# The middle of a decode kernel's feed-forward in two halves, and its second weight in other pieces

## The chip, the cores and the metric

One core of a Trainium2 chip. The metric is the device time of one execution in microseconds (us), the median of several executions. Inside one profiled execution I use a second, finer measure: times counted from the landing of the last part of w1 (the sixteenth semaphore increment of that transfer in the trace), because what the change touches begins there and the 345 us before it differ by some tenths from one execution to the next. These differences are taken in nanoseconds and then rounded; the recorded texts took some of them from rounded times and so stand 0.01 us off in places (1.57 for 1.58, 1.38 for 1.39).

## The reference, cut to what matters

One decode step: an attention block with a cached K and V of 8 heads x 32768 positions x 128 (134 MB in bfloat16, 32 query heads), an output projection, then a feed-forward block:

```python
h = _layernorm(x) * (1 + cb) + sb
x = x + gb * (relu(h @ w1) @ w2)      # w1: 512 x 1792, w2: 1792 x 512
```

The batch is one row, so the feed-forward is two products of one row with a matrix. w2 is 14 "rows" of 512 columns per partition (128 partitions x 14 = 1792); one such row is 128 KB.

Of the kernel before, what the change touches and what calls it, by code (L numbers as in the profile page):

```python
# [11 lines left out]
ACT = mybir.ActivationFunctionType  # L12
# [5 lines left out]
def kernel(  # L18
# [14 lines left out]
    nc = tc.nc  # L33
    P = 128
# [4 lines left out]
    KT = D // P  # L39
    Dff = B_w1.shape[1]  # L40
    FT = Dff // P
# [6 lines left out]
    WOROWS = 2  # L48
    LAST = Hkv - 1
    LOOPED = Hkv - 2  # L50
    W2P = [(0, 4), (4, 8), (8, 10), (10, 12), (12, 13), (13, 14)]
    W1P = [(0, KT - 1), (KT - 1, KT)]
    assert Dh == 128 and REP == 4 and D == 512 and FT == W2P[-1][1] and NTILE == 4
    scale = float(Dh) ** -0.5
# [36 lines left out]
    def piece(name, at, n):  # L91

        if name not in pieces:
            pieces[name] = ring.tile([P, 2 * TK * Dh], BF16, tag="slot", name=name)
        return pieces[name][:, at:at + n]

    def load(key):
# [23 lines left out]
        else:  # L121
            f0, f1 = W2P[key[1]]
            t = piece("w12_sb", KT * Dff + f0 * D, (f1 - f0) * D).rearrange("p (f d) -> p f d", d=D)
# [20 lines left out]
    stream += [("v", LAST, (0, 1)), ("v", LAST, (2,)), ("v", LAST, (3,))] + [("wo", i) for i in range(len(WOP))]  # L144
    stream += [("w1", i) for i in range(len(W1P))] + [("w2", i) for i in range(len(W2P))]
    pos = [0]

    def need(key):
        while key not in loaded:
            load(stream[pos[0]])  # L150
            pos[0] += 1
        return loaded[key]
# [17 lines left out]
    for hp in range(4):  # L170
# [9 lines left out]
        out=mask4, in_=ident_f[:].rearrange("p (x q) -> p q x", q=REP), op=ALU.add, axis=AX.X,  # L180
# [3 lines left out]
    for n in sorted({n * REP for _, n in WOP}):  # L184
        cmask[n] = const.tile([P, P // n], F32, name=f"cmask{n}")
        nc.vector.tensor_reduce(
            out=cmask[n][:], in_=ident_f[:].rearrange("p (c r) -> p c r", r=n), op=ALU.add, axis=AX.X,
# [3 lines left out]
            out=rsel_f[:], in_=ident_f[:].rearrange("p (c r) -> p r c", r=n), op=ALU.add, axis=AX.X,  # L191
# [6 lines left out]
        out=smask[:], in_=ident_f[0:16, 0:16].rearrange("p (s q) -> p s q", q=REP), op=ALU.add, axis=AX.X,  # L198
# [8 lines left out]
        out=place32[:], in_=ident_f[:].rearrange("p (j m) -> p m j", m=32), op=ALU.add, axis=AX.X,  # L207
# [3 lines left out]
        out=rowpick[:], in_=ident_f[:].rearrange("p (j m) -> p j m", m=32), op=ALU.add, axis=AX.X,  # L211
# [10 lines left out]
        out=cx_bd[:], in0=cx_row[:].unsqueeze(1).to_broadcast([16, 8, D // 8]),  # L222
# [17 lines left out]
    def bank(name):  # L240
        return ps_s.tile([P, 512], F32, tag="s", name=name)[:]
# [61 lines left out]
    def rows_sb(name):  # L303
        return spool.tile([P, 2, 512], F32, tag="S_g", name=name)
# [26 lines left out]
    def four_rows(e, name):  # L331
# [15 lines left out]
        out=nca[:], in0=modT_sb[:, KT:2 * KT], scalar1=-1.0, scalar2=-1.0, op0=ALU.mult, op1=ALU.add,  # L347
# [3 lines left out]
        out=ncb[:], in0=modT_sb[:, 4 * KT:5 * KT], scalar1=-1.0, scalar2=-1.0, op0=ALU.mult, op1=ALU.add,  # L351
# [16 lines left out]
    for i in range(2):  # L368
        nc.vector.transpose(out=q_cols[:, i, :], in_=q_ps[i])
        nc.scalar.copy(  # L370
            out=qT_sb[:, 16 * i:16 * (i + 1)], in_=q_cols[:, i, :].rearrange("p (h r) -> p h r", r=32)[:, :, 0],
# [223 lines left out]
    def keep_clock(n):  # L595

        if not spare:
            spare.append(bank("spare_ps"))
        for _ in range(n):
            nc.tensor.matmul(spare[0], lhsT=ident_bf[:], rhs=qbd[0][:, 0, 0:4, :], start=True, stop=True)  # L600

    with tc.manual_schedule(engines={mybir.EngineType.PE, mybir.EngineType.DVE}):
# [11 lines left out]
        for g in range(LAST):  # L614
# [58 lines left out]
        hid_ps = ps_o.tile([P, 512], F32, tag="o", name="hid_ps")  # L673
# [22 lines left out]
            out=x1T[:], in0=x1T[:], scalar=1.0, in1=xT, op0=ALU.mult, op1=ALU.add, accum_out=stat2[:, 0:1],  # L696
# [15 lines left out]
        NQ = 32 * FT  # L712
        for part, (k0, k1) in enumerate(W1P):
            w1_sb = need(("w1", part))
            for kt in range(k0, k1):
                for q in range(4):
# [2 lines left out]
                        rhs=w1_sb[:, kt - k0, q * NQ:(q + 1) * NQ], start=False, stop=(kt == KT - 1),  # L719
                        skip_group_check=True,  # L720
                    )
        keep_clock(4)
        hidT = rows_sb("hidT").rearrange("p a b -> p (a b)")[:, 0:NQ].rearrange("p (f e) -> p f e", e=32)
        nc.vector.transpose(out=hidT, in_=hid_ps[:, 0:NQ].rearrange("p (e f) -> p f e", f=FT))  # L724
        hb = hid_bd[:]
        nc.scalar.activation(  # L726
            out=AP(hb.tensor, hb.offset, [hb.ap[0], [KT * KT, FT], [KT + 1, KT]]),
            in_=hidT[:, :, 0:1].to_broadcast([P, FT, KT]), func=ACT.Relu,
        )

        ffn_ps = bank("ffn_ps")[0:KT, 0:P]
        for part, (f0, f1) in enumerate(W2P):
            w2_sb = need(("w2", part))
# [41 lines left out]
```

## The kernel before: the parts that the change touches

All of K, V and the weights run through one queue of transfers (Sync engine), in the order of use; wo, w1 and w2 come last. w2 comes in six pieces, each a transfer with its own semaphore:

```python
W2P = [(0, 4), (4, 8), (8, 10), (10, 12), (12, 13), (13, 14)]
...
stream += [("w1", i) for i in range(len(W1P))] + [("w2", i) for i in range(len(W2P))]
```

At the end the hidden row lies in PSUM on four partitions. Vector (DVE) turns it so that it lies along partitions, Scalar (ACT) applies the relu and writes the values on diagonals of a zeroed tile, and TensorE (PE) multiplies: four matmuls for each row of w2, 56 in all, into one accumulator. `keep_clock(n)` issues n unused matmuls that keep TensorE busy while it waits.

```python
keep_clock(4)
hidT = ...                                   # 128 x 448, in SBUF
nc.vector.transpose(out=hidT, in_=hid_ps[:, 0:NQ].rearrange("p (e f) -> p f e", f=FT))
nc.scalar.activation(out=AP(hb.tensor, hb.offset, [hb.ap[0], [KT * KT, FT], [KT + 1, KT]]),
                     in_=hidT[:, :, 0:1].to_broadcast([P, FT, KT]), func=ACT.Relu)
ffn_ps = bank("ffn_ps")[0:KT, 0:P]
for part, (f0, f1) in enumerate(W2P):
    w2_sb = need(("w2", part))
    for ft in range(f0, f1):
        for i in range(KT):
            nc.tensor.matmul(ffn_ps, lhsT=hid_bd[:, ft, i, :], rhs=w2_sb[:, ft - f0, i * P:(i + 1) * P], ...)
o_rows = ffn_ps * gb_rows; o_bf = o_rows + x1_rows     # two Vector operations, then the store (abridged)
```

## Time and profile before

| | before |
|---|---|
| time, median of the first 3 runs | 355.47 us (355.39 to 356.15) |
| span of the profiled execution | 353.3 us |
| w1's last landing | 345.62 us from the start |
| last of the 56 matmuls starts | 350.35 us |

The page and the chain of waits are shown in the prediction. Beside them, these are the instructions of the middle in order of time (start, length, engine, line, operation, count; in brackets the idle time before and what ended it; PEld is the loading of weights into TensorE):

```profile
346.07 0.65 DVE L724 STREAM_TRANSPOSE hidT<-hid_ps 128x448 f32<-128x448 f32 x1 [1.32 <-PE hid_ps L717]
346.82 0.33 ACT L726 ACTIVATE hid_bd<-hidT 128x56 bf16<-128x56 f32 x1 [2.71 <-DVE hidT L724]
347.19 3.19 PEld L736 LDWEIGHTS <-hid_bd 128*4 128x4 bf16 x56 [0.70 <-ACT hid_bd L726]
347.19 3.37 PE L736 MATMUL ffn_ps<-w_sb,hid_bd 128*4 128x128 bf16 x56 [0.20 <-ACT hid_bd L726]
```

The matmuls wait for ACT, ACT for DVE.

### The profile page before, as it was taken

Reading aid. Unit: us, or ns where it says so; the run is one execution under the profiler, and the core shown is the slowest. Engines: PE = TensorE matmul, PEld = TensorE weight load, DVE = VectorE, ACT = ScalarE, POOL = GpSimd, SP = SyncE. Lnnn points to the kernel's source line nnn. Section 1 sums busy time; section 2 is a strip of 40 time slices with the busy share of each in tenths; the row PEclk is TensorE's granted clock in tenths of the full one; section 3 lists DMA queues with packets and bytes.
Section 4 is the critical chain, followed back from the end, with each engine's and each line's share of the span. In section 5 each row is a group of like instructions: output and inputs, shape, how many; then the busy total and the mean of one; then the engine's idle time right before and its main releaser. Section 6 shows DMA issues by size and latency. Waiting matters only on the chain. (4 is left out here: it accounts for less than half of the span.)

```text
span 353.3 us, 3999 instructions
## 1 busy us (share of the span) xinstructions
PE 282.0 (80%) x1310; PEld 112.9 (32%) x1312; DVE 209.1 (59%) x270; ACT 28.3 (8%) x68; POOL 9.7 (3%) x16
## 2 busy tenths in 40 slices
PE   0273882899798979897989796979689797989996
PEld 0031331233233323332333232323234233334444
DVE  7737683963848467662939177553938095743141
ACT  1023004000110011001010101010100000011000
POOL 8200000000000000000000000000000000000000
PEclk9985888599899999998999999999969999999999
DMA  8999999999999999999999999999999999999995
GB/s 312 456 419 438 443 420 423 449 434 419 440 441 419 427 456 421 423 449 434 419 438 443 419 423 454 430 418 445 441 415 427 449 428 419 449 438 403 429 419 204
DMA packets 6852, 149.59 MB, mean 423 GB/s; under 512 B 824, under 2 KB 1080, under 8 KB 1976
## 3 DMA queue, kind: packets, MB, share of 16 engines
q1 hardware_dynamic: 6776, 149.43, 98.5%
q8 instruction: 8, 0.13, 0.1%
q14 instruction: 4, 0.03, 0.0%
q0 software_dynamic: 64, 0.00, 0.0%
HBM read 149.42 MB, written 0.00 MB: 423 GB/s over the span
## 5 line engine op out<-in xcount | busy, mean ns | idle before, releaser
L405 DVE STREAM_TRANSPOSE KTt<-Ksb 128x2048 f32<-128x2048 f32 x64 | 143.3, 2284 | 60.6 <-DMA Ksb<-in_A_k_cache_dram 50.4
L487 PE MATMUL o_ps<-Vsb,PT_g 128*16 (+1 forms) x512 | 129.2, 390 | 21.7 <-ACT qbd L389 9.7
L425 PE MATMUL S_ps<-KTt,qbd 128*128 128x512 bf16 x512 | 124.6, 396 | 17.0 <-DVE KTt L405 15.6
L425 PEld LDWEIGHTS <-qbd 128*128 128x128 bf16 x512 | 49.5, 99 | 83.2 <-issue 26.6
L487 PEld LDWEIGHTS o_ps<-Vsb,PT_g 128*16 x416 | 36.9, 89 | 90.2 <-issue 64.6
L431 DVE TENSOR_SCALAR_CACHE_REDUCE S_g<-S_ps 128x512 f32<-128x512 f32 x16 | 11.0, 690 | 30.5 <-PE S_ps L425 30.5
L389 ACT COPY qbd<-qrep_sb 32x128 bf16<-32x128 bf16 x32 | 9.4, 295 | 134.4 <-PE S_ps L425 133.3
L468 DVE STREAM_TRANSPOSE PT_g<-P_g 128x1024 bf16<-128x1024 bf16 x8 | 9.8, 1225 | 6.7 <-ACT P_g L462 6.6
L459 ACT ACTIVATE nbias<-Mb_ps 128x1 f32<-128x1 f32 x8 | 1.4, 171 | 133.1 <-PE Mb_ps L457 133.1
L227 PE MATMUL xc_ps<-cx_sel,cx_bd 16*128 16x2 bf16 x4 | 0.3, 172 | 14.5 <-DVE cx_bd L221 14.5
L487 PEld LDWEIGHTS <-PT_g 128*16 128x16 bf16 x96 | 8.2, 90 | 11.0
L462 ACT ACTIVATE P_g<-S_g,nbias 128x1024 bf16<-128x1024 f32 x8 | 9.2, 1149 | 0.2
L173 DVE COPY sel<-ident_bf 128x128 bf16<-128x128 bf16 x4 | 8.1, 3940 | 1.1 <-POOL ident_bf masks.py:199 1.1
L518 DVE SCALAR_TENSOR_TENSOR Y<-o_ps,smask,Y 16x128 f32<-16x128 f32 x24 | 8.1, 339 | 0.8
L474 PE MATMUL L_ps<-Lexp,ones_f 128*128 128x4 f32 x16 | 2.9, 254 | 4.3 <-DVE Lexp L471 4.3
L446 DVE TENSOR_REDUCE Mrow<-mT_ps 1x4 f32<-1x128 f32 x8 | 2.1, 257 | 7.1 <-PE mT_ps L443 7.1
L600 PE MATMUL spare_ps<-qbd,ident_bf 128*128 128x512 bf16 x18 | 5.4, 380 | 0.2 <-issue 0.2
L443 PE MATMUL mT_ps<-ident_f,m_p 128*1 128x128 f32 x8 | 2.2, 270 | 3.9 <-DVE m_p L440 2.0
L474 PEld LDWEIGHTS L_ps<-Lexp,ones_f 128*128 128x128 f32 x16 | 3.2, 221 | 5.8 <-issue 5.1
L227 PEld LDWEIGHTS <-cx_bd 16*128 16x128 bf16 x4 | 0.2, 114 | 14.5 <-DVE cx_bd L221 14.5
L537 DVE TENSOR_TENSOR oT_sb<-acc_ps,Linv 128x4 bf16<-128x4 f32 x8 | 1.2, 152 | 5.7 <-PE acc_ps L524 5.7
L295 PE MATMUL mod_ps<-wm_sb,siluT 128*1 128x512 bf16 x24 | 3.6, 624 | 1.1 <-DVE siluT L289 1.1
(115 smaller groups left out, 88.3 us busy)
## 6 DMA issues: line engine op xcount, KB each, us to landing
Ksb<-in_A_k_cache_dram SPq DMA_DIRECT2D x16, 4096.0 KB, 27.7
Vsb<-in_A_v_cache_dram SPq DMA_DIRECT2D x15, 4096.0 KB, 24.1
wq_sb<-in_A_wq_dram SPq DMA_DIRECT2D x1, 4096.0 KB, 19.3
Vsb<-in_A_v_cache_dram SPq DMA_DIRECT2D x2, 2048.0 KB, 23.3
wm_sb<-in_w_mod_dram SPq DMA_DIRECT2D x1, 3072.0 KB, 10.1
wo_sb<-in_A_wo_dram SPq DMA_DIRECT2D x1, 2048.0 KB, 24.9
w_sb<-in_B_w_dram SPq DMA_DIRECT2D x1, 1344.0 KB
wo_sb<-in_A_wo_dram SPq DMA_DIRECT2D x1, 1024.0 KB, 27.0
```

What stands on the lines that cost most here:

```text
L173: nc.vector.tensor_copy(out=sel[:, hp, :].rearrange("p (a c) -> p a c", a=4), in_=src)
L295: nc.tensor.matmul(dst[j // 4][32 * (j % 4):32 * (j % 4) + 1, :], lhsT=src_T[:, kt:kt + 1], rhs=w[:, kt, j * 512:(j + 1) * 512], start=(kt ...
L389: nc.scalar.copy(out=o, in_=i)
L405: t = nc.vector.transpose(out=KTt[:].bitcast(F32), in_=Ksb[:, 32 * half:32 * half + 32, :].rearrange("p j d -> p (j d)").bitcast(F32),)
L425: nc.tensor.matmul(S_ps_tiles[g], lhsT=qbd[g % 2][:, hp, s, :], rhs=KTv[:, 16 * sl:16 * sl + 16, h, :, par], start=(t4 == 0 and sl == 0 an ...
L431: nc.vector.tensor_scalar(out=S_tiles[g][:, G, :], in0=S_ps_tiles[g], scalar1=1.0, scalar2=None, op0=ALU.mult, op1=ALU.max, accum_out=m_ti ...
L462: nc.scalar.activation(out=P_g[:], in_=S_g[:].rearrange("p g f -> p (g f)"), func=ACT.Exp, bias=nbias[:], scale=scale, accum_out=l_g[:],)
L468: nc.vector.transpose(out=PT_g[:], in_=P_g[:])
L474: nc.tensor.matmul(L_ps[:], lhsT=ones_f[:], rhs=Lexp[:], start=True, stop=True)
L487: nc.tensor.matmul(o_tiles[g][:], lhsT=PT, rhs=Vx, start=False, stop=False, skip_group_check=True)
L518: nc.vector.scalar_tensor_tensor(out=Y[:], in0=o[:, s], scalar=smask[:, s:s + 1], in1=Y[:], op0=ALU.mult, op1=ALU.add,)
L600: nc.tensor.matmul(spare[0], lhsT=ident_bf[:], rhs=qbd[0][:, 0, 0:4, :], start=True, stop=True)
```

## The change

The intent: DVE and ACT work in two halves, so that the first w2 rows can start while the second half is still being turned; one filler less, because PE is wanted sooner; and w2 in pieces of 4, 3, 3, 2, 1, 1 rows instead of 4, 4, 2, 2, 1, 1, so that the second piece is there sooner.

```diff
-    W2P = [(0, 4), (4, 8), (8, 10), (10, 12), (12, 13), (13, 14)]
+    W2P = [(0, 4), (4, 7), (7, 10), (10, 12), (12, 13), (13, 14)]
...
-        keep_clock(4)
+        keep_clock(3)
...
-        nc.vector.transpose(out=hidT, in_=hid_ps[:, 0:NQ].rearrange("p (e f) -> p f e", f=FT))
+        hid_v = hid_ps[:, 0:NQ].rearrange("p (e f) -> p f e", f=FT)
         hb = hid_bd[:]
-        nc.scalar.activation(
-            out=AP(hb.tensor, hb.offset, [hb.ap[0], [KT * KT, FT], [KT + 1, KT]]),
-            in_=hidT[:, :, 0:1].to_broadcast([P, FT, KT]), func=ACT.Relu,
-        )
+        for f0, f1 in ((0, FT // 2), (FT // 2, FT)):
+            nc.vector.transpose(out=hidT[:, f0:f1], in_=hid_v[:, f0:f1])
+            nc.scalar.activation(
+                out=AP(hb.tensor, hb.offset + KT * KT * f0, [hb.ap[0], [KT * KT, f1 - f0], [KT + 1, KT]]),
+                in_=hidT[:, f0:f1, 0:1].to_broadcast([P, f1 - f0, KT]), func=ACT.Relu,
+            )
```

## The prediction

> **What bounds the kernel now.** I read the page first (busy shares, slices), then the chain of waits, then the timeline of the last 10 us, and last the issue and landing of each w2 piece.
>
> ```profile
> PE 282.0 (80%) x1310; PEld 112.9 (32%) x1312; DVE 209.1 (59%) x270; ACT 28.3 (8%) x68; POOL 9.7 (3%) x16
> ...
> PEclk9985888599899999998999999999969999999999
> DMA  8999999999999999999999999999999999999995
> ```
> The line of DMA shares is at nine tenths or more in nearly every slice; no compute engine is. The kernel is a stream of 149 MB at 423 GB/s, and everything before the last weight rows hides behind it. Only the last slice (8.8 us) is thinner: the stream ends there. The change touches nothing but that tail, so I read the tail of the chain of waits (start, length, what):
>
> ```profile
> 322.32 23.30 DMA w_sb<-in_B_w_dram
> 345.62 0.04 issue
> 345.66 0.39 PE hid_ps L717 x4
> ...
> 346.07 0.66 DVE hidT L724
> ...
> 346.82 0.34 ACT hid_bd L726
> 347.15 0.04 issue
> 347.19 3.39 PE ffn_ps L736 x56
> 350.58 0.02 issue
> 350.61 0.29 DVE o_rows L741
> 350.90 0.02 issue
> 350.92 0.28 DVE o_bf L743
> ```
> Read as it stands, it says: the last part of w1 lands at 345.62, four matmuls make the hidden row, DVE turns it (0.66), ACT puts it on the diagonals (0.34), 56 matmuls follow without a named wait (3.39), then two DVE operations and the store. That invites the sum "a quarter microsecond off DVE and ACT is a quarter microsecond off the end". It holds only if the 56 matmuls may all move forward, and each piece of w2 has to be in memory first. So I took the issue of the second piece (rows 4 to 7), the third (rows 8 and 9) and the last (row 13), each with its time to landing:
>
> ```profile
> 331.56 0.33 SPq L133 DMA_DIRECT2D w_sb<-in_B_w_dram  x1
> DMA to landing us min/median/max: 16.6/16.6/16.6
> ...
> 336.41 0.33 SPq L133 DMA_DIRECT2D w_sb<-in_B_w_dram  x1
> DMA to landing us min/median/max: 12.4/12.4/12.4
> ...
> 341.35 0.33 SPq L133 DMA_DIRECT2D w_sb<-in_B_w_dram  x1
> DMA to landing us min/median/max: 8.7/8.7/8.7
> ```
> That is 331.56 + 16.6 = 348.2, 348.8 and 350.1. The trace's semaphore records give the sixteenth increment of the six pieces more finely: 346.87 (rows 0 to 3), 348.13 (4 to 7), 348.78 (8, 9), 349.41 (10, 11), 349.75 (12), 350.08 (13). The matmuls that need them start at 347.19, 348.175, 349.07, 349.51, 349.96 and 350.18. So w2 is landing while it is used: the last piece has 0.10 us to spare, and the second has none. Matmul 16 starts at 348.030 and matmul 17 at 348.175, 145 ns later, where the others stand 56 ns apart: about 0.09 us of waiting that no view lists as idle, because every matmul record lasts 219 ns and overlaps the next.
>
> ```profile
> L736 PE MATMUL ffn_ps<-w_sb,hid_bd 128*4 128x128 bf16 x56 | 3.4, 219 | 0.2 <-ACT hid_bd L726 0.2
> ```
> The reader should see that "idle 0.2 <- ACT" is one wait ahead of the whole group and that the wait for DMA inside it is invisible here.
>
> **What the Trainium skill says.** "DMA: Bandwidth & Descriptors", section "Why a DMA increments its semaphore by 16 and not by 1": a transfer runs on up to 16 DMA engines that finish independently, and only the full 16 means that the data has landed. The trace agrees: the sixteen increments of the second w2 piece run from 346.39 to 348.13, so the slowest engine decides, 1.7 us behind the first. "TensorE: Matmul & The Clock Gate", section "Wait — 56ns, not 53.3ns?": 128 columns warm measure 55.6 ns start to start; the trace has 55.8. "VectorE: DVE Perf Modes", section "The TRN2 errata — SBUF-src ops pay a fixed extra latency per instruction": reading PSUM costs a fixed 120 cycles plus one per element at 0.96 GHz, hence 592 ns for the 448-wide turn; the trace has 650, so I take the page's slope and the trace's base. "ScalarE: Activation LUTs", section "Rules for kernel authors": some 0.3 us per ACTIVATE plus 0.83 ns per element; 56 elements give 0.35, the trace has 0.326.
>
> **The change part by part.** (1) The turn: one of 448 elements a partition becomes two of 224. Half the elements are 224/0.96 = 233 ns less, so the first half takes 650 - 233 = 417 ns, ending at 346.07 + 0.42 = 346.49. (2) ACT starts 94 ns after the turn's end now (346.722 to 346.816), so at 346.58; 28 elements fewer cost 326 - 28 x 0.83 = 303 ns, ending at 346.89. PE starts 50 ns after ACT's end now, so at 346.94: 0.25 us earlier than 347.19. (3) The second halves: DVE ends near 346.9, ACT starts near 347.0 and ends near 347.3; row 7, the first that needs it, is not due before 346.94 + 7 x 0.223 = 348.50 (four matmuls of 55.8 ns a row). The built order shows that PE waits for ACT once more only there and that the second DVE half waits for nothing. So one DVE and one ACT instruction more, both hidden: 0. (4) One filler matmul less: its slots are 216 ns apart, so the fillers end near 346.77 instead of 346.99. With four of them PE would come to w2 about 0.05 us after ACT. (5) w2 in 4, 3, 3, 2, 1, 1: issues wait for older transfers on the same eight semaphores and stay put; bytes and order of rows stay too. The second piece is one row shorter: 4 rows lay 348.13 - 346.87 = 1.26 us apart, 0.315 a row, so it lands at 347.82. The third ends with the same row as before: 348.78. The rest is unchanged.
>
> Now the matmuls run against the landings, with 45 ns from sixteenth increment to first matmul (348.13 to 348.175). Rows 0 to 3 from 346.94 to 347.83. Rows 4 to 6 from max(347.83, 347.82 + 0.045) = 347.87 to 348.54. Rows 7 to 9 cannot start before 348.78 + 0.045 = 348.825: a wait of 0.29 us, and they last to 349.49. Rows 10, 11 (landed 349.41) to 349.94, row 12 to 350.16, row 13 (landed 350.08) to 350.385. Before, the same count from 348.175 with ten rows gives 348.175 + 40 x 0.0558 = 350.405. Gain: 0.02 us. With nothing to wait for, the end would be 346.94 + 56 x 0.0558 = 350.06, a gain of 0.34. And even with every other wait away, row 13 alone holds the end at 350.08 + 0.045 + 4 x 0.056 = 350.35: the most that this tail can give is 0.055 us. So the 0.25 us become a wait ahead of row 7 in place of the ones removed.
>
> **The rivals.** (A) The landings set the end, as worked out: 355.47 - 0.02 = 355.45, at most 355.41. For it: the landings above. (B) The full gain: the landings were late in this one execution, or the stream ends earlier now, and PE follows ACT: 355.47 - 0.25, or 0.34 with the hidden wait, so 355.1 to 355.2. Against it: nothing in the change makes bytes come sooner, and PE's wait before matmul 17 shows it caught up with the stream already. (C) The stream is disturbed: 3 KB rows a partition in place of 4 and 2 KB, or a landing later by some tenths, which then goes one for one into the end: 355.6 to 355.8. Against it: the pieces of 2 rows landed 0.315 us a row apart, the pieces of one row 0.33, as the one of four rows, so size hardly matters. (D) The clock: one filler fewer leaves PE idle and the clock falls to half in the 56 matmuls, which would add 56 x about 53 ns = 3 us. Against it: the gap from the last filler's end to the first w2 matmul is 0.20 us now and 0.17 after, and the granted clock is 1.00 in every half microsecond from 345 to 353. (E) Half-turned data makes the first ACT wait for both turns: then no gain in step 2, and 355.45 to 355.5 because the stream hides it.
>
> **Range and chances.** The estimate is 355.45 us, from A with a small share of B and C. What spreads it is not the change but the runs: three of before span 355.39 to 356.15, and the median of a few runs elsewhere may lie some tenths off. So 355.05 to 355.90 for 8 in 10: below by B plus scatter, above by C or one long run in the median. A gain over 2% would be 7 us, more than the whole tail after 346.07 could give without stopping the stream: 0.004. A loss over 2% would need D twice over or a slow state: 0.004. Within 2%: 0.992.
>
> **What the profile would show.** Step 1: two turns of about 0.42 us, the first from 346.07 relative to w1's landing at 345.62. Step 2: first w2 matmul 1.32 us after w1's last landing in place of 1.57. Step 3: no wait for ACT in the middle. Step 5: the second piece landing about 0.3 us sooner against w1, the third and the last unchanged (3.16 and 4.46 us after w1's last landing). The sum: the 56 matmuls last about 3.6 us instead of 3.39, with a step of about 0.3 us before matmul 29 and almost the same end. It would be wrong if the last matmul ended more than 0.1 us sooner after w1's last landing, if the landings moved against each other, or if PE's clock fell.

## The result, and the profile after

The changed kernel took 355.37 us (median of 6 runs, 355.18 to 355.60), the kernel before 355.52 in 6 runs (355.28 to 356.15). The ratio is 0.9994, with a 95% interval from 0.9981 to 1.0007. A ratio here is the mean time of one kernel's runs over that of the other's of the same rounds, in the experiments without each one's profiled run, so not quite the ratio of the medians. No difference is shown, and the 0.15 us between the medians lies inside the scatter of either kernel.

The tail of the chain of waits in the changed kernel (start, length, what):

```profile
336.71 12.38 DMA w_sb<-in_B_w_dram
349.09 0.04 issue
349.13 1.74 PE ffn_ps L738 x28
350.87 0.02 issue
350.89 0.29 DVE o_rows L743
```

The chain no longer runs through DVE and ACT. It goes from the last 28 matmuls straight to a transfer: the third piece of w2, issued at 336.71 and landed at 349.09. Matmul 29, the first of row 7, starts at 349.13. The middle itself became shorter, as it should (the same view as before, in order of time):

```profile
346.35 0.71 DVE L727 STREAM_TRANSPOSE hidT<-hid_ps 128x224 f32<-128x224 f32 x2 [1.33 <-PE hid_ps L717]
346.86 0.50 ACT L728 ACTIVATE hid_bd<-hidT 128x28 bf16<-128x28 f32 x2 [2.48 <-DVE hidT L727]
347.25 1.63 PEld L738 LDWEIGHTS <-hid_bd 128*4 128x4 bf16 x29 [0.70 <-ACT hid_bd L728]
347.28 3.57 PE L738 MATMUL ffn_ps<-w_sb,hid_bd 128*4 128x128 bf16 x56 [0.23 <-DMA w_sb<-in_B_w_dram]
349.13 1.53 PEld L738 LDWEIGHTS <-hid_bd 128*4 128x4 bf16 x27 [0.25 <-issue]
```

The stretch of the 56 matmuls went from 3.37 to 3.57 us. The weight loads show where: they fall into two groups, 29 and 27 (one load runs ahead of its matmul), with 0.25 us of idle time between. In this trace w1's last landing is at 345.90 (345.62 before), so I subtract it:

| us after w1's last landing | before | changed |
|---|---|---|
| first w2 matmul starts | 1.58 | 1.39 |
| step before matmul 17 (row 4), start to start | 145 ns | 71 ns |
| step before matmul 29 (row 7) | 56 ns | 332 ns |
| w2 pieces land at | 1.25, 2.51, 3.16, 3.79, 4.13, 4.46 | 1.25, 2.25, 3.19, 3.79, 4.12, 4.47 |
| last w2 matmul starts | 4.73 | 4.74 |

PE starts 0.19 us sooner and ends 0.01 us later. All that the middle gave is handed back as waiting ahead of row 7. (That the changed kernel's profiled execution lasts 353.6 us and not 353.3 comes from ahead of the tail: w1 landed 0.28 us later in it.)

### The profile page after: what moved, and what is told of

Its sections match the earlier page's. It is cut to its first block, busy times and chain, and to the rows that moved or that the text cites. A ratio compares the mean times of both kernels' runs of the same rounds, so it can differ in the third digit from the quotient of the medians.

```text
span 353.6 us, 4001 instructions
## 1 busy us (share of the span) xinstructions
PE 281.5 (80%) x1311; PEld 112.5 (32%) x1311; DVE 209.2 (59%) x271; ACT 28.4 (8%) x69; POOL 9.7 (3%) x16
## 5 line engine op out<-in xcount | busy, mean ns | idle before, releaser
L425 PE MATMUL S_ps<-KTt,qbd 128*128 128x512 bf16 x512 | 123.0, 391 | 18.5 <-DVE KTt L405 17.2
L362 PE MATMUL q_ps<-wq_sb,hT 128*1 128x512 bf16 x32 | 3.6, 623 | 1.2 <-DVE hT L278 1.2
```

The source lines that it names most:

```text
L362: nc.tensor.matmul(q_ps[i][32 * a:32 * a + 1, :].rearrange("o (h e) -> o h e", e=32), lhsT=hT[:, kt:kt + 1], rhs=wq_f[:, kt, i, a], start= ...
L425: nc.tensor.matmul(S_ps_tiles[g], lhsT=qbd[g % 2][:, hp, s, :], rhs=KTv[:, 16 * sl:16 * sl + 16, h, :, par], start=(t4 == 0 and sl == 0 an ...
```

## The experiments

**Theory 1**: the landings of w2 set the end, so a shorter middle is only waited away. **Theory 2**: the split makes its own new wait: row 7 is also the first row that needs the second ACT half, and PE's program waits for ACT a second time just there. The step before matmul 29 would then be the fault of the split and not of the transfer. **Theory 3**: the gain is real and hidden in the scatter of the runs, or something else (the clock, after one filler less) eats it.

Each table row below is one profiled execution; "w1 group" is the start of the last four w1 matmuls, all times in us after w1's last landing; steps are start to start, 56 ns being normal.

| kernel | w1 group | first w2 matmul | steps | row 13 landed | last matmul |
|---|---|---|---|---|---|
| before | 0.04 | 1.58 | 145 ns at 17 | 4.46 | 4.73 |
| changed | 0.04 | 1.39 | 71 at 17, 332 at 29 | 4.47 | 4.74 |
| split_only | 0.04 | 1.38 | 377 at 17 | 4.46 | 4.77 |
| pieces_only | 0.62 | 2.15 | none | 4.46 | 5.22 |
| pieces_only2 | 0.04 | 1.58 | 153 at 29 | 4.47 | 4.74 |
| thin_before | 0.04 | 1.58 | none | 2.05 | 4.65 |
| thin_after | 0.25 | 1.49 | none | 2.04 | 4.56 |
| thin_after2 | 0.15 | 1.39 | none | 2.05 | 4.46 |
| slow_middle | 0.04 | 1.62 | 108 at 29 | 4.47 | 4.74 |
| row_more | 0.04 | 1.39 | 70 at 17, 623 at 29 | 4.77 | 5.03 |
| seven | 0.04 | 1.39 | 111 at 33, 255 at 41, 109 at 53 | 4.54 | 4.75 |
| no_fillers | 0.66 | 1.90 | none | 4.47 | 4.97 |
| late_before | 1.71 | 3.25 | none | 4.47 | 6.32 |
| late_after | 0.57 | 1.81 | none | 4.46 | 4.88 |

The last column is what the time hangs on: in 13 of the 14 traces the profiled span ends 2.97 to 2.98 us after the last w2 matmul starts (in seven 3.33, see below). So a gain there would be a gain in the span of that execution. What scatters between executions lies ahead of it: w1's last landing comes anywhere from 345.61 to 346.06 us in these traces, which is more than any gain at stake.

### Each half of the change alone

split_only:

```diff
-    W2P = [(0, 4), (4, 7), (7, 10), (10, 12), (12, 13), (13, 14)]     # changed kernel
+    W2P = [(0, 4), (4, 8), (8, 10), (10, 12), (12, 13), (13, 14)]
```

> The middle in two halves and three fillers, but w2 in the old pieces of 4, 4, 2, 2, 1, 1 rows. All times from the last landing of w1. Theory 1 (the landings of w2 set the end): first w2 matmul at 1.38 us as in the changed kernel; the second piece lands at 2.51, so the step moves from matmul 29 to matmul 17 and is about 0.33 us (0.28 of it waiting); none at 29; last matmul starts at 4.73, as in both kernels; time within 0.1 us of before. Theory 2 (the second ACT half, for which PE waits ahead of row 7, makes the step): the step of about 0.33 us stays at matmul 29. Theory 3 (no wait binds, the gain is there and only lost in the scatter of runs): last matmul starts at 4.45 or earlier.

Measured: 355.70 us median of 5 (before 355.45 in 9), ratio 1.0001 (0.9988 to 1.0015). The step is at matmul 17, 377 ns (the second piece landed at 2.55, not 2.51), and there is none at 29. Its chain of waits names the transfer of the second piece in place of the third:

```profile
332.00 16.59 DMA w_sb<-in_B_w_dram
348.60 0.04 issue
348.64 2.41 PE ffn_ps L738 x40
```

The ACT halves are the same two instructions as in the changed kernel, yet the step followed the boundary between pieces. Theory 2 falls. So does theory 3's number: the last matmul starts at 4.77, not at 4.45.

pieces_only is the opposite: the kernel before with the new list of pieces and nothing else.

```diff
-    W2P = [(0, 4), (4, 8), (8, 10), (10, 12), (12, 13), (13, 14)]     # kernel before
+    W2P = [(0, 4), (4, 7), (7, 10), (10, 12), (12, 13), (13, 14)]
```

> The middle whole as before, four fillers, w2 in the new pieces of 4, 3, 3, 2, 1, 1 rows. Theory 1: first w2 matmul at 1.57 us after w1's last landing; the second piece lands at about 2.25, so the small step of 145 ns before matmul 17 goes; the third lands at 3.19, so a step of about 150 ns comes before matmul 29; last matmul starts at 4.74. Theory 2: no step at matmul 29, as ACT has one instruction only, and the last matmul starts at 4.65. Time within 0.1 us of before by either.

Measured: 355.49 us median of 5, ratio 0.9996 (0.9981 to 1.0010). The profiled execution was not the one I had counted on: PE came to the last w1 group 0.62 us after its landing and not 0.04 (more on this below), so w2 had landed before PE needed it and no step is there. It tells theories 1 and 2 apart in nothing. I ran it again for one look:

> The kernel before with the new pieces once more, as in its first trace PE came 0.6 us late to w1. Theory 1 where PE is in time: no step before matmul 17, about 150 ns before matmul 29, last matmul at 4.74. Theory 2: no step at 29.

This time PE was in time: 153 ns before matmul 29, none before 17, last matmul at 4.74, 355.21 us in its one run. Both numbers are theory 1's. A step at 29 without any second half shows once more that it belongs to the piece.

### The landings out of the way

thin_before and thin_after load only the first row of each piece and let all its rows use that one; the result is wrong, the instructions on PE, DVE and ACT are the same.

```diff
-            t = piece("w12_sb", KT * Dff + f0 * D, (f1 - f0) * D)...; src = w2_v[:, f0:f1]
+            t = piece("w12_sb", KT * Dff + f0 * D, D)...;             src = w2_v[:, f0:f0 + 1]
...
-                        ffn_ps, lhsT=hid_bd[:, ft, i, :], rhs=w2_sb[:, ft - f0, i * P:(i + 1) * P],
+                        ffn_ps, lhsT=hid_bd[:, ft, i, :], rhs=w2_sb[:, 0, i * P:(i + 1) * P],
```

> The kernel before, with each w2 piece loading only its first row, which all rows of the piece use (wrong result on purpose): the same instructions, 8 rows of w2 less to load, so that no matmul has to wait for a landing. Theory 1: first w2 matmul at 1.57 us after w1's last landing, no step, last at 4.64 (55 x 55.8 ns later): 0.09 us less than before.

> The changed kernel with the same thin w2 (wrong result on purpose). Theory 1: with the landings out of the way the split pays what it saves in the middle: first w2 matmul at 1.27 us after w1's last landing (PE then follows ACT), no step, last at 4.34: 0.30 us less than the thin kernel before, and the time 0.3 us less too, 0.4 less than before. Theory 2: a step before matmul 29 stays and the last matmul starts near 4.6. Theory 3: the same gap of 0.3 us between the thin pair as between the full pair.

thin_before came out as expected to within a hundredth (first 1.58, last 4.65, no step). thin_after had no step either, which is against theory 2 again, but PE was 0.25 us behind w1's landing, so the last matmul started at 4.56 and not 4.34.

> The thin changed kernel once more, as in its first trace PE came late to w1 (last w1 group 0.25 us after the landing). Theory 1: where PE is in time, first w2 matmul at 1.27 us after w1's last landing, last at 4.34, against 4.64 in the thin kernel before; where it is late again, 1.24 us after the last w1 group starts, and 55 x 55.8 ns from there.

0.15 us behind this time; first matmul 1.24 us after the last w1 group (1.39 - 0.15), last at 4.46. Its chain, beside that of thin_before:

```profile
345.66 0.39 PE hid_ps L717 x4
346.05 0.02 issue
346.07 0.66 DVE hidT L724
...
346.82 0.34 ACT hid_bd L726
347.15 0.04 issue
347.19 3.30 PE ffn_ps L736 x56
```

```profile
345.23 0.94 PE hid_ps L717 x16
346.17 0.02 issue
346.19 0.43 DVE hidT L727
...
346.70 0.27 ACT hid_bd L728
346.98 0.04 issue
347.02 3.30 PE ffn_ps L738 x56
```

With nothing to wait for, the 56 matmuls take 3.30 us in both, and the middle from the end of w1's matmuls on is 0.43 + 0.27 in place of 0.66 + 0.34. From the last w1 group to the first w2 matmul it is 1.24 us in both thin changed traces against 1.54 in thin_before (1.58 - 0.04): 0.29 us before rounding, the split's true size. The median times did not show it. thin_before took 355.29 (ratio 0.9992, 0.9978 to 1.0005), thin_after 355.30 (0.9990, 0.9977 to 1.0004), 5 runs each. That miss of the expected 0.3 us stays; part of it can be that PE comes late in some runs of either, and that w1's landing scatters by more than 0.3 us, but only the profiled ones tell. Two of those can be compared: in thin_before and thin_after2 w1 landed at the same time (345.62 and 345.63 us), the last matmul starts at 350.26 and 350.09, and the spans are 353.24 and 353.07, so the 0.17 us won at the last matmul are in the span. That is one execution of each, so I count the thin pair as shown in the traces and not in the medians.

### Moving the middle and moving the landing

slow_middle writes the first half of the diagonals twice, which makes the middle longer; row_more loads row 6 a second time within the third piece (which then lies in a spare place), which makes that piece and all behind it land later and touches no compute instruction.

```diff
+            for _ in range(2 if f0 == 0 else 1):          # slow_middle
                 nc.scalar.activation(...)
```
```diff
             src = w2_v[:, f0:f1]
+            if (f0, f1) == (7, 10):                       # row_more
+                t = piece("w12_sb", KT * Dff + FT * D, 4 * D)...
+                src = w2_v[:, 6:10]                       # row 6 of it is not used
```

> The changed kernel with the first half of the diagonals written twice over on ACT (same result), so that the first w2 matmul comes later. Theory 1: first w2 matmul at about 1.60 us after w1's last landing instead of 1.38, the step before matmul 29 shrinks from 332 to about 120 ns, the last matmul starts at 4.74 as before: 0.2 us lost in the middle cost nothing. If the middle set the end (theory 3) the last matmul comes 0.2 us later, at 4.95.

> The changed kernel with one row more in the third piece (row 6 is loaded a second time, to a spare place, and not used), so that this piece and all behind it land one row later, about 0.32 us; no instruction on PE, DVE or ACT changes. Theory 1: the step before matmul 29 grows from 332 to about 650 ns and the last matmul starts at about 5.06 us after w1's last landing instead of 4.74, time 0.3 us more. Theory 2: nothing changes on PE.

slow_middle: first matmul at 1.62 (0.24 later than in the changed kernel), step at 29 down from 332 to 108 ns, last matmul at 4.74, 355.25 us (ratio 0.9995, 0.9980 to 1.0011; the runs of before beside these and the next ones: 355.44). A quarter of a microsecond more in the middle cost nothing. row_more: third piece at 3.49 instead of 3.19, step 623 ns, last matmul at 5.03, 355.57 us (ratio 1.0005, 0.9990 to 1.0021). 0.29 us more in the landing came out as 0.29 us at the last matmul; the expected 0.3 us in the time is not shown, the interval holds both it and nothing:

```profile
336.61 12.68 DMA w_sb<-in_B_w_dram
349.29 0.04 issue
349.33 1.74 PE ffn_ps L741 x28
351.07 0.02 issue
351.09 0.29 DVE o_rows L746
```

The 1.74 us of the last 28 matmuls are those of the changed kernel; only the landing moved. These two runs are the plainest evidence for theory 1: with PE in time, the middle has slack and the landing has none.

### The best pieces, and the fillers

```diff
-    W2P = [(0, 4), (4, 7), (7, 10), (10, 12), (12, 13), (13, 14)]
+    W2P = [(0, 4), (4, 6), (6, 8), (8, 10), (10, 12), (12, 13), (13, 14)]     # seven
```

> The changed kernel with w2 in seven pieces of 4, 2, 2, 2, 2, 1, 1 rows, which by theory 1 is the best that the pieces can do: steps of tens of ns only, and the last row's landing (4.47 us after w1's last) binds: last matmul starts at 4.47 + 0.045 + 3 x 0.056 = 4.68, against 4.74 in both kernels. That is 0.06 us, not to be seen in the time. By theory 2 the step at matmul 29 stays.

The step at 29 is gone, the waits lie at the later boundaries, and the last landing binds as expected, but that landing came at 4.54 and not 4.47, and the last matmul at 4.75. The time was 355.65 (ratio 1.0008, 0.9994 to 1.0022). So this is not a version that beats both. In its profiled execution the store is issued at 351.25, like before's (351.23), and yet the span ends at 353.7 and not 353.3. The Sync engine's own waits, first before's, then seven's (who, for what, us in total, times, longest):

```profile
SPq L770 <- DMA out_dram<-o_bf: 0.4, 1, 0.4
```
```profile
SPq L772 <- DMA out_dram<-o_bf: 0.8, 1, 0.8
```

With one transfer more, the store comes to a semaphore that the program's closing waits ask for first. In the trace's records that wait lasts 0.79 us and six more checks follow it, some 60 ns each; in the kernel before these ran while the store was under way. That gives 0.35 us more from the store to the end (2.45 against 2.10).

```diff
-        keep_clock(3)      # ahead of the turned hidden row
+        keep_clock(0)      # no_fillers
```

> The changed kernel without its three filler matmuls ahead of w2. Theory 1: PE's idle time before the first w2 matmul grows by 0.8 us, the clock stays (granted 1.00), the first w2 matmul starts at 1.38 us or a little sooner, last at 4.74. Rival on the clock: w2 matmuls 107 ns apart in place of 56, the last matmul 2 to 3 us later.

355.39 us (ratio 0.9999, 0.9984 to 1.0014). The clock rival falls: PE is idle for 0.9 us ahead of w2, the granted clock is 1.00 in the whole stretch from 348 to 351 us, and the 56 matmuls stand 55.8 ns apart. But the rest of the expectation missed: first matmul at 1.90 and last at 4.97. Again PE had come late to w1, 0.66 us after the landing.

### Executions in which PE comes late

In 5 of the 14 traces PE is behind by more than the usual 0.04 us at the last w1 group (pieces_only, no_fillers, thin_after, thin_after2 and late_before, the last beyond what its extra fillers explain; late_after's 0.57 is what those fillers alone do). They are told apart by one thing far ahead of the tail: the granted clock from 295 to 300 us is 0.50 to 0.68 in these five, and 1.00 in the other nine. By the clock records it is at 0.50 there for 3.4 us in the two thin traces, which are 0.25 and 0.15 us late, and for 6.8 us in the other three, which are 0.6 us late or more. While it lasts, matmuls of 512 columns start 427 ns apart and not 216. The stretches, columns: window, length, busy us (and count) of PE, weight loads, DVE, ACT, POOL, granted clock, DMA share, GB/s; first before, then no_fillers:

```profile
295.00:300.00 5.00, 4.16 (x20) 1.80 (x19) 1.72 (x8) 0.00 (x0) 0.00 (x0) 1.00 0.97 419
```
```profile
295.00:300.00 5.00, 4.34 (x14) 1.85 (x13) 1.74 (x8) 0.00 (x0) 0.00 (x0) 0.55 0.97 419
```

PE does fewer matmuls in the same time, starts the last K scores at 307.4 us in place of 305.7, and from there it, and not the stream, sets the time of the hidden row. The chain of no_fillers shows it: from there to the end it runs through PE, DVE and ACT without a transfer. Its tail:

```profile
345.75 0.94 PE hid_ps L717 x16
346.69 0.02 issue
346.71 0.43 DVE hidT L727
347.14 0.02 issue
347.18 0.04 issue
347.22 0.27 ACT hid_bd L728
347.49 0.04 issue
347.54 3.30 PE ffn_ps L738 x56
```

In such an execution the landings are past when PE arrives, so by theory 1 the split should pay in full. To test that on purpose I held PE back in both kernels:

```diff
+        keep_clock(5)      # late_before, late_after: ahead of the matmuls with w1
         for part, (k0, k1) in enumerate(W1P):
```

> The kernel before with five fillers more ahead of the matmuls with w1, which holds PE back by 5 x 0.216 = 1.08 us there, so that PE and not w1's last landing sets the hidden row's time (as three earlier traces had it by chance). Theory 1: last w1 group about 0.65 us after w1's last landing, first w2 matmul 1.53 us after that (2.2 after the landing), no step among the 56, last matmul at about 5.25.

> The changed kernel with the same five fillers. Theory 1: w2 has landed before PE comes to it, so the split now pays: first w2 matmul 1.24 us after the last w1 group starts, no step, last matmul at about 4.96: 0.29 us sooner than its twin; the time lower by 0.2 to 0.3 us, which the scatter of runs may still cover. If the split cannot pay even there (theory 2: the second half makes PE wait), a step at matmul 29 stays and the last matmul is near 5.25.

From the last w1 group to the first w2 matmul: late_before 1.54 us, late_after 1.24, no step in either; 0.30 us of gain that nothing takes back. late_after's last matmul is at 4.88 (4.96 expected). late_before's profiled execution fell into the low clock as well (0.57), so its whole tail lies 1.1 us later than the fillers alone would put it, and the 1.4 us between the two last matmuls must not be read as the split's work. In time: late_before 356.35 us (ratio 1.0020, 1.0006 to 1.0033), late_after 355.73 (1.0014, 1.0001 to 1.0028), against the same runs of before (355.29). The difference of the ratios, 0.0006, is 0.2 us and has the expected sign, but the intervals overlap, so no gain in time is shown here either.

## Why the prediction was right, point by point

- **The bound.** That w2 lands while it is used, and that a wait of 0.09 us hides in the kernel before because matmul records overlap, held: 145 ns at matmul 17, gone where the piece is smaller (pieces_only2).
- **Step 1, the turn.** Predicted 417 ns, measured 417. The second half starts 340 ns after the first.
- **Step 2, ACT and the first matmul.** ACT's half took 264 ns, not 303, so that term was too large by 39 ns. That did not help: the first matmul came at 1.39 us after w1's landing and not at 1.32. The prediction compared ACT's end with the landing of rows 0 to 3 (1.25) and took that piece for present; in the trace PE waits for that piece, and its first matmul comes 0.135 us after the landing, not 0.045 (0.135 or 0.136 in split_only, row_more and seven too; where the piece had landed before, 0.05 us after ACT's end). So the gain in the start was 0.19 and not 0.25 us. This did not reach the end, as row 7 waited anyway.
- **Step 3, the second halves.** Hidden, as predicted: split_only has no step at row 7.
- **Step 4, the fillers.** Even none of them left the clock at 1.00 in the one trace taken. That a fourth would have held PE back by 0.05 us was not tested.
- **Step 5, the pieces.** Second piece 0.26 us sooner (0.31 predicted), third 0.03 later (3.19 for 3.16), last unchanged within 0.01. The second came later than predicted because its three rows took 0.333 us each and not 0.315. The wait before row 7 was 332 - 56 = 276 ns, predicted 0.29 us.
- **The sum.** Predicted gain at the last matmul 0.02 us, measured -0.01 in the two traces; the difference is the third piece's 0.03 us. Predicted time 355.45 us, measured 355.37, in the range. The time alone proves little: rivals A, B, C and E all lay in that range, and the medians of the kernel before alone run from 355.29 to 355.52. That the number came within 0.08 us is partly luck; that landings and not the middle set the end is shown by the traces.
- **The rivals.** B (the full gain) was set aside with "PE caught up with the stream already". That is so only where PE is in time; in the late executions B is right for the middle (0.30 us). How often they occur in unprofiled runs stays open, and with it whether the 0.15 us between the medians has anything to do with the change. C did not show at the size it named (though in the two kernels' traces rows landed 0.33 to 0.35 us apart in pieces of one row, against 0.31 to 0.32 in those of four), D fell with no_fillers, and E did not occur: ACT's first half starts at 346.86, 0.09 us after the first turn ends and 0.20 before the second does.

Two things stay open. That the low clock at 295 to 300 us causes the lateness is argued from 14 traces that it separates without exception, and from the matmuls at half speed in it; no run set the clock, and why it falls in some executions and not in others is not known. And the thin pair's equal medians are not explained.

## What to carry to other kernels

A chain of waits ends at the last releaser and does not show how closely the others follow: before shortening a step, list when each input of what comes after it lands, and move the whole sequence forward against that list. Here it took one line per piece to see that 0.25 us in the middle could give 0.055 us at most. Here the choice of pieces decided which row waits and hardly when the end comes: the last matmul started at 4.73 to 4.77 us in all six traces with w2 loaded whole, no row added and PE in time.

## What the Trainium skill lacked or had wrong

- "ScalarE: Activation LUTs", section "Rules for kernel authors": by 0.83 ns per element, 28 elements fewer should save 23 ns; this form (a broadcast read, a write at every fifth element) saved 62 (326 to 264 ns in the traces of the two kernels).
- "VectorE: DVE Perf Modes", section "The TRN2 errata — SBUF-src ops pay a fixed extra latency per instruction": the slope of one element per cycle was exact for the PSUM turn (650 - 417 = 233 ns for 224 elements), the level was not that of the records (592 by the formula, 650 measured). Records are not a fair measure of the level, though: two turns back to back start 340 ns apart while the first one's record is 417, and the formula gives an estimate of 358 for 224 elements.
- "Perfetto Trace Analysis", section "DMA Optimizations", gives small DMAs (under 2 KB) a significant overhead per transfer, without saying whether the whole transfer or one partition's run is meant. Here, in a full queue, pieces of 1 KB per partition (128 KB in all) landed 0.335 and 0.338 us a row against 0.312 and 0.316 for 4 KB, some 7%. I found no page with the price of one transfer more in a full queue: with seven pieces the last landing came 0.07 us later (4.47 to 4.54).
- No page says that a wait inside a run of matmuls is invisible as idle time while it is shorter than the overlap of the records: here 219 - 56 = 163 ns; the wait of 89 ns in the kernel before was found only in start-to-start times.
- No page has the order of a program's closing waits: 0.35 us more from the store to the end where the store's semaphore was asked for first (2.45 against 2.10 us).
